# The plain block of a sequence DFT, reordered from re-then-im into two rounds over the halves of d

## The chip, the cores and the metric

The kernel runs on one core of one Trainium2 chip. The metric is the device time of one execution in microseconds, as the median of several runs. The engines are named as the profile names them: PE (TensorE, matmul) with PEld (its weight loads), DVE (VectorE), ACT (ScalarE), POOL (GpSimd) and SP (SyncE, which issues most of the DMAs here).

## The reference

One block of a network on a sequence of S = 2048 tokens with D = 1024 channels, F = 3584 hidden units and one vector c. Every number is f32.

```python
mod = (silu(c) @ w_mod).reshape(1, 6, 1, D)        # w_mod is [1024, 6 * 1024]
sa, ca, ga, sb, cb, gb = (mod[:, i] for i in range(6))
h = layernorm(x) * (1 + ca) + sa
x = x + ga * real(DFT_seq(DFT_hidden(h)))          # two dense DFT matrices, re and im each
h = layernorm(x) * (1 + cb) + sb
x = x + gb * (gelu(h @ w1 + b1) @ w2 + b2)
```

The sequence DFT needs h, and h needs sa and ca, which are two of the six columns of blocks of w_mod: 8 MB of weights stand before the first useful matmul. ga, sb, cb and gb are needed later.

## The kernel before, in words

Every f32 operand of a large product is split into two f16 numbers, a high half and a low half (what the high half misses), and a product is three passes of f16 matmuls, `PASSES = ((0,0),(0,1),(1,0))`, each 128x128 by 128x512. The high half is an ACT copy, the low half a DVE subtraction that waits for it.

The stages follow one another on PE: the plain block of the sequence DFT (its line is L1121, 768 matmuls), then the rest of the sequence DFT in Winograd form (L1171, 2016 matmuls, product operands from DRAM tensors named s and from sums of the planes of c, L725), the hidden DFT (L1403, 1344 matmuls), w1 (L1597) and w2 (L1706), 2352 matmuls each. From 949 us on, w1 and w2 take turns in blocks of 84 to 168 matmuls.

*The plain block* computes, for the first quarter of t, both planes (re and im) of the sequence DFT of all 1024 columns of h. Its loop has 16 steps n = (ri, kp): all eight kp of re, then all eight of im. In a step stand 48 matmuls, for two halves s of the sequence, eight columns of 128 of h (d) and three passes. Eight PSUM banks hold the eight d. A step needs h of row pair kp (rows kp and kp + 8 of the 16 blocks of 128 tokens) and one operand c of 512 KB, split into halves by L690 (ACT) and L693 (DVE). Banks are emptied by ACT at L1100 into a tensor from which the u operands of the hidden DFT are made (sums at L797, high halves at L782, low halves at L785) and stored to DRAM by POOL's queue (L787); u of re is pushed when re is finished, in the middle of the block, and u of im at its end.

*Ahead of it*, sa and ca are made from w_mod by eight loads of 1 MB (`wm2`, loaded at L1436, from SP). Some of them are multiplied on PE with silu(c) broadcast (L482, L483; f32 matmuls), the others by DVE into an accumulator (`mod_dve`, L488, L490), which PE then adds up over the partitions (L496). `mod_rows` finds the largest magnitude (L516), makes a scale from it, and brings the first row block of x to h in two halves (L503, L508; ACT's copies at L521 to L534). `x_tasks` does the same for the other row blocks: the statistics by ACT with an accumulator (L610, L614; each instruction is followed by a read-out of the accumulator), a chain of operations on two columns (L612 to L627), then x minus mean times ca and plus sa over all 1024 columns (L642, L643), the ACT copy (L644) and the low half (L645).

*Beside the block*, `s_tasks` (L652) makes sums and differences of the rows of h over DVE (L656 to L659), splits them (L667, L670) and stores them to s by POOL's DMA queue (L674); they are pushed during im's half. `row_tasks` (L541) does ga, sb, cb and gb: accumulations of 1 MB pieces by DVE (L553), a POOL reduction over the partitions (L561), and a store to a DRAM row by SP (L575), spread over the Winograd blocks. The s operands come back by SP (L752), on the same queue as those stores, as the w_mod loads (L545) and as the loads of c (L714).

*What sets the order.* The kernel is written out by a planner, engine by engine. A piece of work is a `Task` with an engine, an estimated cost, dependencies and a key; `push` puts tasks on named streams with due times, `fill_to(t)` writes out tasks whose estimated end lies before PE's clock, `pick` takes the one that can begin first among those due, and `emitted` and `need` force tasks that the next instruction depends on. `LAGS` and `LANDS` are the delays that the planner adds. The planner's clocks are estimates: on the chip each engine runs its list in order and waits where an operand isn't there. SBUF places are fixed offsets in one tile ("arena"), so a load into a place must wait for the last reader of what was there.

*The w2 operands.* The first w2 block takes seven loads `("w2", 0, m)` of w2's part-products m from DRAM, pushed with tag `w2_0` at L1901 to L1911 in the branch g == 1, and issued by SP at L1907. All seven wait for the z operations (L405, L407, L420) of block NB − 2, whose places they take, and stand behind the stores of w in SP's queue. hid1 is the second half of the hidden activations for that block (`hid_tasks(1)`, L395 on ACT and L407 on DVE).

## Time and profile before

| | us |
|---|---|
| runs | 1980.77, 1979.91, 1982.81 (median 1980.77) |
| the profiled execution's own time | 1980.77 |
| its span in the profile | 1979.0 |
| PE busy | 1950.1 |
| DVE busy | 1426.8 |
| ACT busy | 851.6 |
| POOL busy | 189.3 |
| first matmul of the plain block | 35.39 |
| first matmul of the Winograd part | 209.66 |
| first matmul of the first w2 block | 1010.34 |

How to read it: the span runs from the first to the last recorded event, and the little of the execution that lies outside it is the difference between its own time and the span. Busy times are sums over instructions, so that an engine which is busy for all but a per cent of the span sets the time, and others matter only where it waits for them. A row of the timeline gives start, duration, engine, line, operation, output and inputs, shape and count, and in brackets the idle time of that engine just before, with what ended it. A row of groups gives the busy sum, the mean of one in ns, and the idle time ahead of the group.

### The profile page before, as it was taken

To read this page: it belongs to the slowest core of one execution; us is meant where nothing else is said; L and a number is where in the kernel's file an instruction comes from. 1 tells how busy PE (TensorE), PEld (TensorE's weight loads), DVE (VectorE), ACT (ScalarE), POOL (GpSimd) and SP (SyncE) were. 2 spreads that over 40 slices of the span, in tenths; PEclk is the share of its full clock that TensorE was granted. 3 is DMA by queue.
4 is the path that set the end of the run, shared out by engine and by line. 5 is a ranking of instruction groups with operands and counts; after the bars stand their busy time and mean duration, and the time that the engine had idled before them with its cause. 6 is when DMAs were issued, how large, how long until landed. Compare 5 with 4: busy or idle time off the path is not lost.

```text
span 1979.0 us, 23588 instructions
## 1 busy us (share of the span) xinstructions
PE 1950.1 (99%) x9004; PEld 887.6 (45%) x9004; DVE 1426.8 (72%) x1799; ACT 851.6 (43%) x1091; POOL 189.3 (10%) x282
## 2 busy tenths in 40 slices
PE   7999999999999999999999999999999999999999
PEld 2444444444444444444444444444444444444443
DVE  5977886898984477776689998989873453553566
ACT  4743432445542255554577466456323312312311
POOL 0012211221210012211020000000000000000000
PEclk8999999999999999999999999999999999999999
DMA  9147588688688867878765455344476432432323
GB/s 386 61 163 269 193 283 301 227 331 313 239 287 323 307 230 263 280 239 307 294 216 192 155 182 176 124 159 168 175 222 201 123 102 75 129 102 68 112 75 85
DMA packets 139362, 402.41 MB, mean 203 GB/s; under 512 B 15536, under 2 KB 15536, under 8 KB 134640
## 3 DMA queue, kind: packets, MB, share of 16 engines
q1 hardware_dynamic: 112528, 309.92, 45.6%
q0 software_dynamic: 26720, 90.98, 13.0%
q8 instruction: 70, 1.15, 0.2%
q14 instruction: 44, 0.36, 0.1%
HBM read 262.95 MB, written 137.89 MB: 203 GB/s over the span
## 4 chain that ended last, share of the span: by engine, by line
PE 83%; DVE 10%; DMA 5%; issue 1%; ACT 1%; SPq 0%; DVEq 0%; POOL 0%; ACTq 0%; POOLq 0%
PE ps L1597 24%; PE ps L1706 24%; PE ps L1171 14%; PE ps L1403 14%; PE ps L1121 5%; DVE arena L693 2%; DMA arena<-in_wm_dram 2%; DVE arena L642 1%; DVE arena L643 1%; DMA arena<-s 1%; DMA arena<-u 1%; DVE arena L797 1%; PE ps L1305 1%; DVE arena L645 1%; DVE arena L725 1%
## 5 line engine op out<-in xcount | busy, mean ns | idle before, releaser
L1706 PE MATMUL ps<-arena 128*128 128x512 f16 x2352 | 512.3, 380 | 5.2 <-DMA arena<-w 4.1
L1597 PE MATMUL ps<-arena 128*128 128x512 f16 x2352 | 510.2, 379 | 0.0
L1171 PE MATMUL ps<-arena 128*128 128x512 f16 x2016 | 435.6, 379 | 1.4 <-DMA arena<-s 1.4
L1706 PEld LDWEIGHTS <-arena 128*128 128x128 f16 x2352 | 230.4, 98 | 284.9 <-issue 7.9
L1597 PEld LDWEIGHTS <-arena 128*128 128x128 f16 x2352 | 230.1, 98 | 276.9
L1752 DVE SCALAR_TENSOR_TENSOR arena<-ps,i4c,arena 128x1024 f32<-128x1024 f32 x179 | 229.3, 1281 | 148.9 <-PE ps L1706 144.3
L1171 PEld LDWEIGHTS <-arena 128*128 128x128 f16 x2016 | 197.1, 98 | 239.8 <-DMA arena<-s 2.4
L1403 PE MATMUL ps<-arena 128*128 128x512 f16 x1344 | 292.4, 379 | 0.9 <-DMA arena<-u 0.9
L395 ACT ACTIVATE arena<-arena,shc 128x512 f16<-128x512 f32 (+1 forms) x115 | 116.2, 1018 | 282.6 <-PE ps L1706 190.9
L1403 PEld LDWEIGHTS <-arena 128*128 128x128 f16 x1344 | 131.4, 98 | 157.0 <-DMA arena<-u 1.4
L1121 PE MATMUL ps<-arena 128*128 128x512 f16 x768 | 169.3, 382 | 9.0 <-ACT arena L526 3.9
L420 DVE TENSOR_TENSOR arena<-arena 128x512 f32<-128x512 f32 (+1 forms) x228 | 171.0, 753 | 4.1
L690 ACT ACTIVATE arena<-arena 128x1024 f16<-128x1024 f32 x100 | 104.1, 1050 | 147.3 <-PE ps L1171 110.0
L407 DVE SCALAR_TENSOR_TENSOR arena<-arena,shc 128x512 f16<-128x512 f32 (+1 forms) x115 | 128.6, 1122 | 35.0 <-ACT arena L395 34.6
L693 DVE SCALAR_TENSOR_TENSOR arena<-arena 128x1024 f16<-128x1024 f32 x100 | 128.7, 1304 | 18.9 <-ACT arena L690 18.9
L1623 DVE TENSOR_TENSOR arena<-arena,ps 128x512 f32<-128x512 f32 x84 | 57.6, 685 | 111.8 <-PE ps L1597 107.6
L1616 ACT ACTIVATE arena<-arena,b1s,i1c 128x512 f32<-128x512 f32 x84 | 68.3, 813 | 137.1 <-DVE arena L1623 137.1
L1121 PEld LDWEIGHTS <-arena 128*128 128x128 f16 x768 | 75.2, 98 | 103.5 <-issue 5.6
L782 ACT ACTIVATE arena<-arena 128x1024 f16<-128x1024 f32 x56 | 57.8, 1048 | 60.9 <-DMA u<-arena 21.8
L395 ACT ACTIVATE arena<-arena,s1c 128x512 f16<-128x512 f32 (+1 forms) x70 | 60.7, 884 | 42.3 <-DVE arena L420 30.1
L785 DVE TENSOR_TENSOR arena<-arena 128x1024 f16<-128x1024 f32 x56 | 66.9, 1218 | 14.8 <-ACT arena L782 14.8
L407 DVE SCALAR_TENSOR_TENSOR arena<-arena,s1c 128x512 f16<-128x512 f32 (+1 forms) x70 | 66.2, 959 | 11.3 <-ACT arena L395 11.2
(161 smaller groups left out, 1392.3 us busy)
## 6 DMA issues: line engine op xcount, KB each, us to landing
w<-arena SPq DMA_DIRECT2D x64, 512.0 KB, 4.5
arena<-w SPq DMA_DIRECT2D x119, 256.0 KB, 2.7
u<-arena POOLq DMA_DIRECT2D x56, 512.0 KB, 5.1
arena<-u SPq DMA_DIRECT2D x112, 256.0 KB, 4.1
arena<-w SPq DMA_DIRECT2D x56, 512.0 KB, 3.5
arena<-s SPq DMA_DIRECT2D x48, 512.0 KB, 7.7
arena<-in_cre_dram SPq DMA_DIRECT2D x32, 512.0 KB, 6.8
arena<-in_cim_dram SPq DMA_DIRECT2D x32, 512.0 KB, 5.8
```

What stands on the lines that cost most here:

```text
L395: act.activation(o[m][0], q(j), AF.Copy, **sc)
L407: dve.scalar_tensor_tensor(o[m][1], q(j), scale, o[m][0], op0=ALU.mult, op1=ALU.subtract)
L420: dve.tensor_tensor(q(d), q(a), q(b), op=op)
L690: h = Task("act", 1.15, lambda: act.activation(o[:, :, 0], s2, AF.Copy, scale=SC), list(deps) + free)
L693: dve.scalar_tensor_tensor(o[:, :, 1], s2, SC, o[:, :, 0], op0=ALU.mult, op1=ALU.subtract)
L1121: pe.matmul(bank_of(d_), hleft(d_, s, kp, a), cop(n)[:, s, b], start=(kp == 0 and s == 0 and a == 0 and b == 0), stop=(kp == 7 and s == 1 ...
L1171: pe.matmul(bank_of(st + ch), left, cop(n)[:, s, b], start=(start and kp == 0 and s == 0 and a == 0 and b == 0), stop=(kp == 3 and s == 1 ...
L1403: pe.matmul(bank_of(bk), up(N)[:, c_, a], dp(n)[:, c_, w], start=(start and ri == 0 and c_ == 0 and i == 0), stop=(ri == 1 and c_ == 3 and ...
L1597: pe.matmul(ps.rearrange("p (k t) -> p k t", k=4), w1c[:, m, s, a, d * P : (d + 1) * P], zc(m)[:, b, :, d, :], start=(start and d == 0 and ...
L1616: act.activation(dst, src, AF.Gelu_apprx_tanh, scale=inv, bias=b1s[:, 2 * p + j : 2 * p + j + 1])
L1706: pe.matmul(t[:, j], hidc[:, c_, m, a, k * P : (k + 1) * P], w2c[:, m, c_, w], start=(start and c_ == 0 and n == 0), stop=(c_ == 1 and n = ...
L1752: lambda: dve.scalar_tensor_tensor(dst, ps[b], inv, dst, op0=ALU.mult, op1=ALU.add), kp[b],
```

## The change

It has two parts that don't touch one another.

1. The plain block runs in two rounds q = 0, 1, one per half of d. In a round every kp is passed with re (banks 0 to 3) and im (banks 4 to 7), 24 matmuls each, kp from 0 to 7 in round 1 and from 7 to 0 in round 2. Both rounds need c of re and im: there are places for 10 more than before, and three kp (six operands) are loaded and split again in round 2, so 22 c operands instead of 16. h is made by halves: `h_tasks(k, q)` for each half of the columns. w_mod's sa and ca columns are loaded by halves of d too (512 KB pieces with runs of 2 KB): the first half before the first matmul, as before but with its own scale, the second half by `mod_tasks`, in round 1: eight loads, eight DVE accumulations (L508, L510), a POOL reduction and a chain that ends in the second scale. The evictions multiply by a scale that depends on the half (`esc`). Statistics (`stat_tasks`) are separate from h, and ACT makes them for row pair 0 too. The s operands are made in round 2 (`s_tasks`, kp from 7 to 0), and u of re and im follow the block, im 50 us after re by the planner's due times. 32 dummy f16 matmuls on a constant tile (`idle_pe`), in five groups, stand on PE between the mod matmuls and the first real one. The planner's start time T0 is 23 instead of 42.
2. w2's first operands are pushed one stage sooner (g == 0). Load m = 0 waits for nothing of z(NB − 2), m = 1 for it, and those with m > 2 for hidden activations of the last block; two of z(NB − 2)'s places move to offsets 28 and 30 and one to 196, and hid1's tenth task waits for z(NB − 2). A load of gb waits for both z.

The core of the diff:

```diff
+    def load_wm2(k, q):
+        dst = wm2(k, q).rearrange("p (c d) -> p c d", c=2)
+        sp.dma_start(dst, wm[:, k, 0 : 2 * D].rearrange("p (c h d) -> p c h d", c=2, h=2)[:, :, q, :])
+    def idle_pe(n):
+        w = ones.bitcast(F16)
+        for _ in range(n):
+            pe.matmul(mbank(5), w[:, 0:P], w[:, 0:512], start=True, stop=True)
...
+    def mod_tasks():
+        t = []
+        for k in range(ND):
+            l = Task("dma", 1.3, lambda k=k: load_wm2(k, 1), [("m1", k - 4)] if k > 3 else [], ("wm1", k))
+            t.append([l])
+            f = lambda k=k: mod_dve(mrow, k, 1, k == 0)
+            t.append([Task("dve", 1.3, f, [l.key] + ([("m1", k - 1)] if k else []), ("m1", k))])
...
+        c_ = chain(
+            ("pool", 7.0, lambda: gp.partition_all_reduce(mrow, mrow, P, RED.add)),
+            ("dve", 0.4, one),
+            ("dve", 3.2, top),
+            ("act", 0.65, lambda: act.activation(sas[:, H[1]], mrow[:, H[0]], AF.Copy, scale=sh(1))),
+            ("act", 0.65, lambda: act.activation(ca1s[:, H[1]], mrow[:, H[1]], AF.Copy, scale=sh(1))),
+        )
...
-        t[0].deps = (("h", k, 0), ("h", k, 1), ("op", 4))
+        t[0].deps = (("h", k, 0, 1), ("h", k, 1, 1))
...
-        b = at(O_AUX + 4 * (n % 4), 1024)
+        b = at(32 + 4 * ((7 - n) % 8) if n < 16 else O_AUX + 4 + 4 * (n % 2), 1024)
...
+        f = lambda: act.activation(uf[:, ri, q, c_], bank_of(4 * ri + c_), AF.Copy, scale=esc(ri, q))
...
-        for n in range(16):
-            ri, kp = divmod(n, 8)
-            steps = [(d, s) for s in range(2) for d in range(ND)]
+        for q in range(2):
+            for kp in (range(8), range(7, -1, -1))[q]:
+                all_ = [(d, s) for s in range(2) for d in range(4)]
...
+                    units += [(q, kp, ri, all_) for ri in range(2)]
+        for q, kp, ri, steps in units:
...
-            if n % 8 == 7:
+            if q and last:
                 d = [[("ev", 0, ri, 4 * h + k) for k in range(4)] for h in range(2)]
-                push("u", "u", u_tasks(0, ri, d), clk["pe"] + 40.0 + 20.0 * ri)
+                push("u", "u", u_tasks(0, ri, d), clk["pe"] + (0.0,50.0)[ri])
...
+    order = [("w", k) for k in range(3)] + [("x", 0)] + [("w", k) for k in range(3, 8)] + [("c", 0), ("x", 8), ("c", 1)]
+    order += [("x", 1), ("x", 9), ("c", 2), ("c", 3), ("x", 2), ("x", 10), ("c", 4), ("c", 5)]
...
+    for k in range(7, -1, -1):
+        push("h1", "x", h_tasks(k, 1), t_two(k) - 12.0)
+        push("s", "s", s_tasks(k), t_two(k)+4.0)
...
+    for k in range(3, 8):
+        if k == 4:
+            push("ml", "ml", wl)
+        push("xl", "xl", [load_x(k), load_x(k + 8), c0[2 * k][0], c0[2 * k + 1][0]])
...
-        return at((O_W if b == NB - 1 else 144) + 4 * n, 1024)
+        return at(O_W + 4 * n if b == NB - 1 else 196 if (b, n) == (NB - 2, 0) else 144 + 4 * n, 1024)
...
+                push("w2l", "w2_0", [Task("dma", 1.5, w2_f(m), [("kept", NB - 1, 0)] if m > 2 else [("z", NB - 2, j) for j in range(7)] if m == 1 else [], ("w2", 0, m)) for m in (0, 1, 2, 4, 3, 6, 5)], due[4, 0] - 10.0)
...
-                push("hid", "hid1", hid_tasks(1), due[4, 0])
+                h1 = hid_tasks(1)
+                h1[9].deps += tuple(("z", NB - 2, m) for m in range(7))
+                push("hid", "hid1", h1, due[4, 0])
```

402 lines of the change are left out of this document (207 added, 195 removed).

## Prediction, written before the changed kernel had been run

> **What bounds the kernel now.** I read the page's first line and section 1, then TensorE's rows in the timeline. The run in which the profile was taken lasted 1980.77 us beside a span of 1979.0, so 1.77 us lie around the span; its time is also the median of the three runs, so the sum is made against 1980.77 directly.
>
> ```profile
> span 1979.0 us, 23588 instructions
> PE 1950.1 (99%) x9004; PEld 887.6 (45%) x9004; DVE 1426.8 (72%) x1799; ACT 851.6 (43%) x1091; POOL 189.3 (10%) x282
> ```
>
> TensorE is busy for all but 1979.0 − 1950.1 = 28.9 us, and the change leaves the count of real matmuls as it is (768 in the plain block in either order). So only two things can move the end: a gap on PE, or a stretch in which PE runs at half pace. The timeline shows where these are (columns: start, duration, what, then idle time before and its releaser):
>
> ```profile
> 35.39 1.16 PE L1121 MATMUL ps<-arena 128*128 128x512 f16 x2 [3.86 <-ACT arena L526]
> 37.66 6.60 PE L1121 MATMUL ps<-arena 128*128 128x512 f16 x23 [0.20 <-DVE arena L503]
> ...
> 52.67 62.75 PE L1121 MATMUL ps<-arena 128*128 128x512 f16 x290 [1.07 <-DVE arena L693]
> ...
> 209.66 93.40 PE L1171 MATMUL ps<-arena 128*128 128x512 f16 x432
> 304.24 119.31 PE L1171 MATMUL ps<-arena 128*128 128x512 f16 x552 [1.18 <-DMA arena<-s]
> 987.95 18.29 PE L1597 MATMUL ps<-arena 128*128 128x512 f16 x84
> 1010.34 38.18 PE L1706 MATMUL ps<-arena 128*128 128x512 f16 x168 [4.09 <-DMA arena<-w]
> 1048.35 36.42 PE L1597 MATMUL ps<-arena 128*128 128x512 f16 x168
> ```
>
> There are three places. The start: no matmul of the DFT before 35.39. The plain block: the pace is 36.42/168 = 0.217 us a matmul (0.2158 from start to start), so 768 take 165.7 us, but the block lasts 209.66 − 35.39 = 174.3; it loses 8.6. The first w2 block: 4.09 us of waiting for its operands, and then 38.18 instead of 36.42 for the same 168 matmuls, a loss of 1.8 to the clock, which had fallen in the gap. A gap of 1.07 (at 52.67) leaves the pace alone, one of 3.86 (at 35.39) is followed by 23 matmuls in 6.60 us (5.0 at full pace).
>
> The other engines, by stretch (columns: PE, PEld, DVE, ACT and POOL busy, then clock, DMA share, GB/s):
>
> ```profile
> 53.00:118.00 65.00, 63.55 (x295) 28.48 (x293) 62.22 (x87) 41.58 (x62) 1.27 (x1) 1.00 0.21 66
> 118.00:210.00 92.00, 92.00 (x428) 41.70 (x427) 64.48 (x70) 40.54 (x48) 21.31 (x39) 1.00 0.72 242
> 209.66:304.24 94.58, 93.40 (x434) 42.18 (x432) 79.03 (x62) 34.05 (x34) 17.19 (x10) 1.00 0.72 253
> 1067.00:1084.60 17.60, 17.60 (x83) 7.95 (x82) 17.43 (x21) 14.83 (x20) 0.00 (x0) 1.00 0.64 207
> ```
>
> In the first half of the plain block DVE is all but full (62.22 of 65): a block that asks for h and c sooner finds no free DVE there.
>
> **Step 1, the start.** Half of w_mod (512 KB pieces) is loaded before the first matmul instead of all of it (1 MB pieces).
>
> ```profile
> 7.13 3.36 PE L483 MATMUL ps<-arena 128*128 128x512 f32 x4 [7.13 <-DMA arena<-in_wm_dram]
> 9.57 1.29 DVE L488 TENSOR_SCALAR arena<-arena,scol 128x2048 f32<-128x2048 f32 x1 [8.13 <-DMA arena<-in_wm_dram]
> 12.04 2.35 DVE L490 SCALAR_TENSOR_TENSOR arena<-arena,scol 128x2048 f32<-128x2048 f32 x1 [1.18 <-DMA arena<-in_wm_dram]
> 28.31 1.06 ACT L690 ACTIVATE arena<-arena 128x1024 f16<-128x1024 f32 x1 [0.70 <-DMA arena<-in_cre_dram]
> 28.99 0.69 DVE L516 TENSOR_REDUCE mx<-ps 128x1 f32<-128x512 f32 x1 [0.59 <-PE ps L496]
> 34.70 0.63 ACT L526 ACTIVATE arena<-arena 128x512 f16<-128x512 f32 x1 [0.96 <-DVE arena L508]
> 37.64 0.75 DVE L508 SCALAR_TENSOR_TENSOR arena<-arena,xcl 128x512 f32<-128x512 f32 x1
> ```
>
> Two 1 MB pieces that DVE waits for come 12.04 − 9.57 = 2.47 apart, so 512 KB take 1.24 us. PE's first matmul waits for piece 0 until 7.13 in the trace of before, so piece 0's first half is there at about 5.9. Piece 7 is the ninth transfer (x0 lies between): 5.9 + 8 × 1.24 = 15.8; c0 follows at 17.1, x8 at 18.3. I take it that the new runs of 2 KB keep this rate, as the c0 load, which has runs of that length, already does (it ends ACT's wait at 28.31, in its turn). The accumulations of 0.75 per 512 columns, in their place between x0's statistics, end at about 18.9. Then ACT, in this order, brings half of x0 to its mean and scale (0.63, to 19.75), makes c0's high half (1.06) and adds up x8 (1.06 and 0.19, rows below). The small DVE operation that takes that sum stands ahead of the first reduction on DVE, so it is what ends last: 19.75 + 1.06 + 1.25 = 22.1. Then two reductions and two sums over 512 columns (4 × 0.6 from start to start) and four operations on one column (about 0.2 each) give the scale at D0 = 25.3. An ACT copy of 0.63 follows, and the first real matmul runs at **26.1 instead of 35.39**: 9.3 us earlier. Twelve of the 32 dummy matmuls run just before it, so it starts at full pace.
>
> **Step 2, round 1.** Here this head start is spent. In a round each kp takes 48 × 0.2158 = 10.36 us for re and im together, and needs a new h (halves of d) and two new c operands. Before, it needed whole h and one c in that time. The price list, per 1024-wide row:
>
> ```profile
> L693 DVE SCALAR_TENSOR_TENSOR arena<-arena 128x1024 f16<-128x1024 f32 x20 | 24.1, 1217 | 0.0
> L643 DVE SCALAR_TENSOR_TENSOR arena<-arena,xcl 128x1024 f32<-128x1024 f32 x15 | 19.2, 1282 | 0.3
> L645 DVE TENSOR_TENSOR arena<-arena 128x1024 f16<-128x1024 f32 x15 | 18.3, 1223 | 3.5 <-ACT arena L644 3.5
> L627 DVE SCALAR_TENSOR_TENSOR xcl<-xcl,m 128x2 f32<-128x2 f32 x7 | 1.5, 219 | 0.1
> L614 ACT ACTIVATE arena<-arena,xcl 128x1024 f16<-128x1024 f32 x14 | 16.0, 1142 | 0.2
> L610 ACT ACTIVATE arena<-arena 128x1024 f16<-128x1024 f32 x12 | 12.6, 1047 | 0.2
> L614 ACT ACTIVATION_READ_ACCUMULATOR arena<-arena,xcl 128x1 f32 x14 | 2.6, 187 | 0.0
> 329.12 7.01 POOL L561 PARTITION_ALL_REDUCE arena<-arena  x1 [34.12 <-DVE arena L553]
> 330.08 5.56 DVE L725 TENSOR_TENSOR arena<-arena 128x1024 f32<-128x1024 f32 x1
> ```
>
> A kp now costs DVE 4 half-wide operations (0.73 each), one low half of h and two of c (1.14 each from start to start), and some eight small ones: 7.5 us of 10.36. ACT has 8 to 8.5 (four statistics of 1.2 with their read-outs, three copies of 1.0, a root). That fits. What does not is the second half of w_mod, which stands in the same round: eight accumulations of about 1.21, and one POOL reduction over 1024 columns. While such a reduction runs in the trace of before, a DVE operation with two SBUF operands takes 5.56 instead of 1.21: DVE stands for 4.35 us. Its first piece can't be worked on before it lands; it is the 36th transfer, 5.9 + 35 × 1.24 = 49.4 = D0 + 24.1.
>
> Counting DVE's new order from D0, four h's matter. The low half of kp 1's h is there at D0 + 16.7 (12 us of work, the rest waits for ACT's statistics); kp 2's stands behind two accumulations, 24.1 + 2 × 1.21 + 1.14 = 27.7. By kp 3's, seven accumulations lie ahead (8.5), two low halves of h and one of c (3.4), four half-wide operations (2.9) and a dozen small ones (2.4): 24.1 + 17.2 = 41.3. To kp 4's come three low halves of c (3.4), one accumulation (1.2), five half-wide operations (3.6), one low half (1.1), small ones (2) and the POOL reduction (4.35): 41.3 + 15.7 = 57. From there PE still has four kp: 57 + 4 × 10.36 = 98.5. Kp 1 alone would allow 16.7 + 72.5 = 89, kp 3 93, kp 5 (63.6) 95. Unhindered the round would end at D0 + 83.7; so about 14.8 us of gaps arise, more than twice those of before.
>
> Round 2 takes 82.9 us. Statistics and w_mod are done by then, the s operands (ACT 1.05, DVE four half adds and 1.22 twice, stores on POOL) move into it, and I see 8.5 to 9.5 us of DVE per kp against 10.36, behind h that is ahead by about 10: no gap. The 82.9 us hold two 4-bank groups whose evictions lie behind the other group's matmuls. The block then ends at 25.3 + 98.5 + 82.9 = 206.7 against 209.66: **−3.0**. The unknown in it is DVE's order: if no small operation waits, kp 4 is ready 2 sooner; if ACT's copies come late behind statistics, 3 later. Range for the block's end: 203.5 to 209.5.
>
> On the gaps: the one before 35.39 was 3.86 and cooled the clock, that of 1.07 did not. Those I expect before kp 1, 3 and 4 are 2.5 to 3.5, in between. One that cools costs 1.6 on the 23 matmuls that took 6.60 and 0.7 on the two ahead of them, which took 1.16: about +2.4, inside the range. The Trainium skill ("TensorE: Matmul & The Clock Gate", "What's actually happening") says that the clock falls to half after an idle window of about 3.4 us that runs free of the program, and rises after as much work; the rows at 35.39 and 1010.34 agree, and it speaks against the change, since by it each of these gaps might, or might not, cool: 209.1 for the block's end with one. The page "SBUF — State Buffer" of the Trainium skill ("Who interferes with whom") has the lock, and would let the whole reduction of 7.01 block DVE; the row at 330.08 shows 4.35, and by the page the end would be 2.7 later.
>
> **Step 3, behind the block.** Before, u of re was made during im's half; now u of re and im come after the block. The trace before has seven u low halves and four sums of re inside the block:
>
> ```profile
> arena<-s SPq DMA_DIRECT2D x48, 512.0 KB, 7.7
> L785 DVE TENSOR_TENSOR arena<-arena 128x1024 f16<-128x1024 f32 x7 | 8.3, 1217 | 0.0
> L797 DVE TENSOR_TENSOR arena<-arena 128x1024 f32<-128x1024 f32 x4 | 4.9, 1218 | 0.0
> 243.77 0.33 SPq L575 DMA_DIRECT2D row_ga<-arena  x1
> 256.47 0.33 SPq L752 DMA_DIRECT2D arena<-s  x1
> 295.03 0.33 SPq L575 DMA_DIRECT2D row_sb<-arena  x1
> 296.10 1.15 SPq L752 DMA_DIRECT2D arena<-s  x1
> ```
>
> About 12 us of DVE work land in a stretch with 94.58 − 79.03 = 15.6 free. It just fits: cost between −1.2 (the present gap at 304.24 goes, because row_sb's store, for which the s load behind it on SP waited, moves back in SP's order) and +12 (rival D). The nearest row is that gap of 1.18; I take +0.5.
>
> **Step 4, w2's first operands.** m = 0 is no longer behind z and is loaded with w1's, so it lies in SBUF when w1's first block ends at 1006.24. m = 1 still waits for z of the second last block:
>
> ```profile
> 1004.30 0.68 DVE L405 TENSOR_TENSOR arena<-arena 128x512 f16<-128x512 f32 x1
> 1005.01 9.84 SPq L1907 DMA_DIRECT2D arena<-w  x7
> 1006.30 1.28 DVE L407 SCALAR_TENSOR_TENSOR arena<-arena,shc 128x1024 f16<-128x1024 f32 x1
> ```
>
> z is done at 1004.98, SP issues at 1005.01, and the first operand released PE at 1010.34: 5.3 us. Now 24 matmuls of m = 0 (5.2 us) lie in that time. The low half of hid1 that they need is done at 1007.58, so 1.3 of the wait stay. 4.09 + 1.8 − 1.3 = **−4.6**; I take −4.5 (at least −3, if m = 1 is 1.5 late; at most −5.8, if hid1 is early too).
>
> **Sum:** −3.0 + 0.5 − 4.5 = −7.0, so 1980.77 − 7.0 = **1973.8 us**. Own range: −3.0 within +3 and −3, the others within +1.3 and −2: about 1969 to 1978.5.
>
> **Rivals.**
> - **B, round 1 isn't starved.** If the mod operations find their place in DVE's free time, the gaps of 14.8 shrink to about 5 and the block ends at 197: 1980.77 − 12.7 + 0.5 − 4.5 = 1964. For it: 7.5 of 10.36 per kp. Against it: 62.22 of 65 in the present half.
> - **C, w2's gain is given back.** DVE has 17.43 of 17.60 at 1067 to 1084.6; if DVE, not PE, sets the pace to there, the earlier start only becomes a wait in the next w2 block: 1980.77 − 3.0 + 0.5 = 1978.3. For it: that row. Against it: DVE's queue moves forward with hid1 as well.
> - **D, slower.** Place: SP's queue in the first Winograd block. Two s loads (for the fifth product operand) stand behind row_ga's store there, which waits for DVE's last operation on that row; that operation moves behind u of re and im. The third load is needed after 14 groups of 24 matmuls, 72.5 us after the block's start, and lands some 7.7 after issue: if DVE gets to the row later than 64 us after the block's start (34 now, 243.77 − 209.66), PE stands for the excess. 34 + 12 leaves 18 of slack; with the whole u work and w_mod's waits ahead of it, 76 would be a stall of 12: 1973.8 + 12 = 1986.
>
> **How the numbers follow.** Forecast 0.45, B 0.22, C 0.13, D 0.20. About 0.2%, 4 us, is what a measurement of this kernel tells from no change: faster is below 1976.8, slower above 1984.7. Faster: 0.40 of the forecast's 0.45 and all of B, 0.62. Same: the rest of the forecast 0.05, C 0.13 and 0.02 of D, 0.20. Slower: 0.18. The range reaches down over B, to 1961, and up to 1984, which leaves out most of D and a little of B.
>
> **What would show it.** First real matmul at 26.1 (step 1); gaps on PE before kp 1, 3 and 4, released by DVE's low halves, with the largest sum in round 1, and a DVE operation of 5.5 us beside POOL's reduction (step 2); no gap in round 2, and the first Winograd matmul at 206 to 207; no gap over 2 us between there and 304 (step 3), else D; the first w2 matmul about 1.3 after w1's last, and m = 1 without a wait (step 4); no new wait for DVE in the w2 block after it, else C. The forecast is wrong most easily in step 2, by the count of DVE's work between D0 and kp 4.

## The result and the profile after

The changed kernel is slower: 1991.51 us in the median of five runs (1988.72 to 1992.79) against 1981.65 of before (1979.91 to 1982.81), a ratio of 1.0043 with a 95% interval of 1.0031 to 1.0055. The profiled execution took 1991.13 us beside a span of 1989.4; the span of before is 1979.0, so the traces differ by 10.4 us, and that is the sum to be explained.

The first line and section 1 of the page of after:

```profile
span 1989.4 us, 23674 instructions
PE 1948.3 (98%) x9006; PEld 885.5 (45%) x9006; DVE 1450.9 (73%) x1868; ACT 868.0 (44%) x1116; POOL 196.8 (10%) x283
```

PE has as much to do as before (1948.3 against 1950.1: 17.9 us instead of 23.7 ahead of the plain block, and more in slow stretches behind gaps), and stands 41.1 instead of 28.9 us. DVE has 24 us more. Where PE stands, the timeline of after shows (start, duration, what, idle time before and its releaser):

```profile
25.41 5.50 PE L1148 MATMUL ps<-arena 128*128 128x512 f16 x24 [1.33 <-ACT arena L1517]
...
39.42 0.61 PE L1148 MATMUL ps<-arena 128*128 128x512 f16 x2 [2.49 <-ACT arena L656]
40.68 10.53 PE L1148 MATMUL ps<-arena 128*128 128x512 f16 x48 [0.66 <-DVE arena L657]
54.65 11.79 PE L1148 MATMUL ps<-arena 128*128 128x512 f16 x46 [3.43 <-DVE arena L657]
...
69.00 11.99 PE L1148 MATMUL ps<-arena 128*128 128x512 f16 x47 [2.00 <-DVE arena L706]
...
83.88 124.06 PE L1148 MATMUL ps<-arena 128*128 128x512 f16 x574 [1.47 <-DVE arena L657]
207.78 52.18 PE L1199 MATMUL ps<-arena 128*128 128x512 f16 x241
260.92 36.42 PE L1199 MATMUL ps<-arena 128*128 128x512 f16 x168 [0.96 <-DVE arena L706]
301.08 12.21 PE L1199 MATMUL ps<-arena 128*128 128x512 f16 x48 [3.74 <-DVE arena L706]
316.04 88.00 PE L1199 MATMUL ps<-arena 128*128 128x512 f16 x407 [2.75 <-DVE arena L706]
409.74 194.04 PE L1199 MATMUL ps<-arena 128*128 128x512 f16 x888 [5.70 <-ACT arena L1218]
605.51 57.15 PE L1199 MATMUL ps<-arena 128*128 128x512 f16 x264 [1.73 <-DMA arena<-s]
662.50 77.86 PE L1431 MATMUL ps<-arena 128*128 128x512 f16 x360
...
1020.94 2.75 PE L1759 MATMUL ps<-arena 128*128 128x512 f16 x12
1025.31 33.85 PE L1759 MATMUL ps<-arena 128*128 128x512 f16 x156 [1.61 <-DMA arena<-w]
1058.99 36.42 PE L1650 MATMUL ps<-arena 128*128 128x512 f16 x168
```

L1148 is the plain block, L1199 the Winograd part, L1431 the hidden DFT, L1650 and L1759 are w1 and w2. Set against the rows of before (its hidden DFT begins at 646.54), stage by stage:

| stage | before, us | after, us | difference | predicted |
|---|---|---|---|---|
| up to the first matmul of the plain block | 35.39 | 25.41 | −10.0 | −9.3 |
| plain block | 174.3 | 182.4 | +8.1 | +6.3 |
| Winograd part | 436.9 | 454.7 | **+17.8** | +0.5 |
| hidden DFT to the end of w1's third block | 359.7 | 358.4 | −1.3 | 0 |
| first w2 block with its wait | 42.1 | 38.05 | −4.1 | −4.5 |
| the rest of the span | 930.6 | 930.4 | −0.2 | 0 |

These are single executions. In the traces of w2_alone, before_plus24 and before_op_2, which start like before, the first matmul runs at 37.6 to 38.2, so the first row is good to some 3 us. The Winograd part repeats better: 436.9 in w2_alone, and 454.5 and 456.2 in mod_quarter and mod_no_wait, which leave it as it is in after.

Everything but one line is within 2 us of the prediction. The Winograd part, whose matmuls the diff leaves as they are, takes 17.8 us more: 14.9 us of gaps and the slow stretches behind two of them (48 matmuls in 12.21 instead of 10.36 at 301.08, 888 in 194.04 instead of 191.6 at 409.74) against 1.4 us of gaps before.

What DVE does ahead of the gap at 301.08, in the timeline of after:

```profile
288.25 1.28 DVE L569 SCALAR_TENSOR_TENSOR arena<-arena,scol 128x1024 f32<-128x1024 f32 x1 [3.19 <-DMA arena<-in_wm_dram]
...
292.55 1.28 DVE L569 SCALAR_TENSOR_TENSOR arena<-arena,scol 128x1024 f32<-128x1024 f32 x1 [1.88 <-DMA arena<-in_wm_dram]
...
297.22 2.67 DVE L569 SCALAR_TENSOR_TENSOR arena<-arena,scol 128x1024 f32<-128x1024 f32 x2
299.81 1.22 DVE L706 SCALAR_TENSOR_TENSOR arena<-arena 128x1024 f16<-128x1024 f32 x1
```

L569 accumulates pieces of w_mod for the row sb, which nothing needs for hundreds of us. Twice DVE stands because a piece hasn't landed, 5.1 us in all, and the low half of an operand (L706), for which PE has stood since 297.3, is queued behind them. A few us on, the gap at 316.04 has the other cause; POOL's rows and DVE's, in the timeline of after:

```profile
309.21 7.28 POOL L577 PARTITION_ALL_REDUCE arena<-arena  x1
```

```profile
310.56 7.70 DVE L706 SCALAR_TENSOR_TENSOR arena<-arena 128x1024 f16<-128x1024 f32 x3
```

Three operand splits, 3.5 us of work, take 7.70 beside the reduction of row sb. The largest gap, 5.70 ahead of 409.74, comes by way of ACT. PE waits for an eviction (L1218, at 408.60), which ACT does behind copies of u (L796) that wait for DVE's sums of u (L811). DVE had stood 2.8 us for pieces, ahead of 385.93 and 388.27, and then beside the reduction of row gb:

```profile
390.61 5.56 DVE L811 TENSOR_TENSOR arena<-arena 128x1024 f32<-128x1024 f32 x1
```

So there are two suspects, waits for pieces (W) and the stand beside reductions (L), and a third, that DVE simply has too much to do (B). The kernel before had the same pieces and the same reductions, and no such gaps. Its DVE even stood longer for pieces, 30.0 us between 208 and 424 where it is 14.3 in after, and once for 10 us on end:

```profile
308.11 0.75 DVE L551 TENSOR_SCALAR arena<-arena,scol 128x1024 f32<-128x1024 f32 x1 [10.20 <-DMA arena<-in_wm_dram]
```

### The profile page after: what moved, and what is told of

It is laid out like the page before. It is cut to its first block, busy times and chain, and to the rows that moved or that the text cites. A ratio compares the mean times of both kernels' runs of the same rounds, so it can differ in the third digit from the quotient of the medians.

```text
span 1989.4 us, 23674 instructions
## 1 busy us (share of the span) xinstructions
PE 1948.3 (98%) x9006; PEld 885.5 (45%) x9006; DVE 1450.9 (73%) x1868; ACT 868.0 (44%) x1116; POOL 196.8 (10%) x283
## 4 chain that ended last, share of the span: by engine, by line
PE 82%; DVE 8%; DMA 6%; issue 2%; ACT 2%; SPq 0%; POOL 0%; DVEq 0%; ACTq 0%; POOLq 0%
PE ps L1759 24%; PE ps L1650 23%; PE ps L1431 15%; PE ps L1199 13%; PE ps L1148 6%; DMA arena<-in_wm_dram 3%; DVE arena L706 2%; DVE arena L569 1%; DVE arena L739 1%; DVE arena L408 1%; PE ps L1333 1%; DMA arena<-s 1%; DVE arena L510 1%; DVE arena L811 0%; DVE arena L799 0%
## 5 line engine op out<-in xcount | busy, mean ns | idle before, releaser
L1759 PE MATMUL ps<-arena 128*128 128x512 f16 x2352 | 510.8, 379 | 2.7 <-DMA arena<-w 1.6
L1650 PE MATMUL ps<-arena 128*128 128x512 f16 x2352 | 510.2, 379 | 0.0
L1199 PE MATMUL ps<-arena 128*128 128x512 f16 x2016 | 440.0, 381 | 14.9 <-DVE arena L706 7.5
L1759 PEld LDWEIGHTS <-arena 128*128 128x128 f16 x2352 | 230.0, 98 | 281.2 <-issue 3.1
L1650 PEld LDWEIGHTS <-arena 128*128 128x128 f16 x2352 | 230.1, 98 | 276.9
L1199 PEld LDWEIGHTS <-arena 128*128 128x128 f16 x2016 | 198.1, 98 | 256.6 <-issue 19.6
L1431 PE MATMUL ps<-arena 128*128 128x512 f16 x1344 | 292.2, 379 | 0.0
L1431 PEld LDWEIGHTS <-arena 128*128 128x128 f16 x1344 | 131.5, 98 | 155.9
L1148 PE MATMUL ps<-arena 128*128 128x512 f16 x768 | 171.0, 384 | 12.9 <-DVE arena L657 5.6
L703 ACT ACTIVATE arena<-arena 128x1024 f16<-128x1024 f32 x106 | 109.6, 1049 | 143.8 <-PE ps L1199 103.7
L706 DVE SCALAR_TENSOR_TENSOR arena<-arena 128x1024 f16<-128x1024 f32 x106 | 139.8, 1330 | 33.0 <-ACT arena L703 33.0
L1148 PEld LDWEIGHTS <-arena 128*128 128x128 f16 x768 | 75.2, 99 | 108.6 <-issue 7.2
L796 ACT ACTIVATE arena<-arena 128x1024 f16<-128x1024 f32 x56 | 57.8, 1049 | 85.2 <-DMA u<-arena 38.0
```

Of the source, the lines that this page charges most:

```text
L703: h = Task("act", 1.15, lambda: act.activation(o[:, :, 0], s2, AF.Copy, scale=SC), list(deps) + free)
L706: dve.scalar_tensor_tensor(o[:, :, 1], s2, SC, o[:, :, 0], op0=ALU.mult, op1=ALU.subtract)
L1148: pe.matmul(bank_of(4 * ri + d_), hleft(4 * q + d_, s, kp, a), cop(n)[:, s, b], start=(first and s == 0 and a == 0 and b == 0), stop=(last ...
L1199: pe.matmul(bank_of(st + ch), left, cop(n)[:, s, b], start=(start and kp == 0 and s == 0 and a == 0 and b == 0), stop=(kp == 3 and s == 1 ...
L1431: pe.matmul(bank_of(bk), up(N)[:, c_, a], dp(n)[:, c_, w], start=(start and ri == 0 and c_ == 0 and i == 0), stop=(ri == 1 and c_ == 3 and ...
L1650: pe.matmul(ps.rearrange("p (k t) -> p k t", k=4), w1c[:, m, s, a, d * P : (d + 1) * P], zc(m)[:, b, :, d, :], start=(start and d == 0 and ...
```

## The experiments

The measure in all of them is the length of the Winograd part in the profile, from its first matmul to that of the hidden DFT: 436.9 us before, 454.7 after. The total is named where it was timed in rounds.

**w2_alone**: before, with the second part of the change alone.

> The kernel before with part 2 alone: w2's first operands loaded one stage sooner, the plain block as before. Theory: the two parts are independent, and part 2 is worth what the changed kernel shows between the end of w1's third block and the start of the next w1 block: 42.1 us before, 38.05 after, so -4.1, about 1977.6. Nothing up to 1006 us should move. Rival: part 2 shifts DVE's z and hid work so that the gain is taken back in the following blocks; then within 1 us of before.

Measured: 1978.32 us against 1981.98 of before, ratio 0.998 (0.997 to 0.9989). Its rows at the first w2 block:

```profile
1008.52 2.75 PE L1706 MATMUL ps<-arena 128*128 128x512 f16 x12
1012.46 34.27 PE L1706 MATMUL ps<-arena 128*128 128x512 f16 x156 [1.19 <-DMA arena<-w]
1046.56 36.42 PE L1597 MATMUL ps<-arena 128*128 128x512 f16 x168
```

38.04 us instead of 42.1. The second part is a gain of 4 us by itself, it isn't taken back, and this kernel beats both. The whole loss is the first part's.

**rows_later**: the changed kernel with the row tasks moved back.

```diff
-        push("row", "row", row_tasks(...), t_op(22) + 20.0 + 30.0 * n)
+        push("row", "row", row_tasks(...), t_op(22) + 60.0 + 45.0 * n)
```

> The changed kernel with one thing moved: the due times of the four w_mod row tasks (ga, sb, cb, gb) go from 20 + 30 n to 60 + 45 n us after the plain block's end. Theory B (backlog: DVE enters the Winograd part with some 25 us more work than before and is the bound for 200 us): work that isn't urgent leaves the full stretch, the gaps at 301, 316 and 410 go, the Winograd part shrinks from 454.7 to about 440 us, total 1976 to 1979. Theory S (the second round's s operands or SP's queue come too late, whatever DVE does): the Winograd part stays over 450 us, total 1989 to 1992.

Measured: 1991.32 us (ratio to before 1.0048, 1.0031 to 1.0064), Winograd part 449.9. Neither theory had it: the gaps at 261 to 316 are gone and that of 410 shrank to 0.85, but new ones came:

```profile
208.03 186.64 PE L1199 MATMUL ps<-arena 128*128 128x512 f16 x864
395.53 41.60 PE L1199 MATMUL ps<-arena 128*128 128x512 f16 x192 [0.85 <-ACT arena L1218]
441.60 13.36 PE L1199 MATMUL ps<-arena 128*128 128x512 f16 x48 [4.47 <-DMA arena<-s]
455.94 5.35 PE L1199 MATMUL ps<-arena 128*128 128x512 f16 x24 [0.98 <-DMA arena<-s]
464.71 193.36 PE L1199 MATMUL ps<-arena 128*128 128x512 f16 x888 [3.41 <-DMA arena<-s]
```

So the row work does make the early gaps, and it makes others where it is put. Of the 4.8 us that the part is shorter, 4.2 are lost again behind it: from the hidden DFT's first matmul (657.91) to the first w2 block (1020.52) it takes 362.6 us instead of 358.4.

**rows_later_pool**: the same, with the stores of the rows issued by POOL instead of SP (`gp.dma_start` for `sp.dma_start` in `put`).

> The changed kernel with the row tasks later (60 + 45 n) and their five stores issued from POOL's queue instead of SP's. With the row tasks later alone the gaps up to 410 were gone, but 8.9 us came back at 441 to 465, released by s loads. Theory Q (those s loads stood on SP behind the stores of row gb and gbb, which wait for POOL's reduction and for DVE): the gaps at 441 to 465 go, the Winograd part takes 438 to 442 us, total 1976 to 1980. Theory R (the ring of s loads or the DMA engines are late there anyway): they stay, total 1988 to 1992.

Measured: 1989.22 us (ratio 1.0034, 1.0022 to 1.0047), Winograd part 447.6, with 2.07 at 449.81 and 5.69 at 460.85 left, released by s loads. Theory Q explains little over 2 us: the prediction's rival D (s loads behind row stores on SP) is real, but small, and the rest of that trouble is not the stores' place. Both traces show where it comes from. DVE stands for row gb's last operation (L588), 11.89 us ahead of 438.79 in rows_later and 9.87 ahead of 436.87 in rows_later_pool, because that operation comes behind a reduction of 9.32 us and a transfer. The splits queued behind it are late, the loads of c wait for the places that these splits free, and the s loads stand behind the loads of c in SP's queue.

**rows_narrow**: DVE's work on the rows nearly gone, its waits kept. Seven of eight accumulations run over 16 columns:

```diff
-  dve.scalar_tensor_tensor(mrow, b, scol[:, k : k + 1], mrow, op0=ALU.mult, op1=ALU.add)
+  dve.scalar_tensor_tensor(mrow[:, 0:16], b[:, 0:16], scol[:, k : k + 1], mrow[:, 0:16], op0=ALU.mult, op1=ALU.add)
```

> The changed kernel with the accumulations of ga, sb, cb and gb over 16 of 1024 columns for seven of eight pieces (the rest of those rows is left out); loads, reductions and the order stay. Theory B (backlog): 28 operations of 1.28 us become 0.1 to 0.2, so DVE has about 30 us back in the 200 us after the plain block; the gaps at 301, 316 and 410 go and the Winograd part takes 438 to 442 us. Theory W (DVE stands in its queue for w_mod pieces that land late, 5.3 us to 318 and 8.3 after): the waits stay, so at least the gap at 301 of 3.7 us stays, and the part takes over 446 us.

Measured: 445.9 us. The windows of this run (PE, PEld, DVE, ACT, POOL busy, then clock, DMA share and GB/s) and its PE rows:

```profile
260.00:318.00 58.00, 51.23 (x233) 22.73 (x231) 42.98 (x41) 19.92 (x20) 10.93 (x8) 0.98 0.81 291
```

```profile
299.01 5.34 PE L1199 MATMUL ps<-arena 128*128 128x512 f16 x24 [1.22 <-DVE arena L706]
306.36 5.34 PE L1199 MATMUL ps<-arena 128*128 128x512 f16 x24 [2.01 <-DVE arena L706]
315.24 281.39 PE L1199 MATMUL ps<-arena 128*128 128x512 f16 x1295 [3.54 <-DVE arena L706]
```

Half of the loss came back (8.8 of 17.8 us), which is between the two theories. DVE is busy 43 of 58 us here, and PE still stands 6.8 us for it, with a quarter of DVE's time free. So work has a part in the loss, but the half that is left isn't a want of DVE time: that speaks for waits, W, against B alone.

**lock_short**: the four reductions over 32 of 1024 columns, every instruction in its place.

> The changed kernel with the four POOL reductions of ga, sb, cb and gb over 32 of 1024 columns (the rest isn't reduced); every instruction stays in its place. Theory L (the reductions, during which DVE stands 4.35 us each, make the gaps): the gap of 2.75 at 316 and most of the 5.70 at 410 go, the one of 3.7 at 301 stays; the Winograd part takes about 445 us. Theory B (backlog): the three reductions ahead of 410 give DVE 13 us back, which is worth something at every later gap; 443 to 448 us. By B the gap at 301, which has one reduction ahead of it, must shrink too.

Measured: 441.0 us. The gap at 316 is gone, 2.94 at 301.29 and 0.70 at 307.33 are left, and that of 410 is gone too. That is more than either theory had.

**no_piece_wait** and **no_wait_no_lock**: seven of the eight accumulations of each row read `mrow` in place of the piece `b`, so that only a row's first piece is still waited for (0.8 us of waits up to 320 in the first run, 2.1 in the second); the second has the short reductions too.

> The changed kernel in which seven of the eight accumulations of each of ga, sb, cb and gb read the row that they add to instead of the w_mod piece (the pieces are loaded and not used, so those rows are left out); the order, the size of every DVE operation, the traffic and the reductions stay, and only the wait for a piece's landing goes. The run with the 12 us of u work off DVE gave back 2.1 us in the Winograd part (452.6 instead of 454.7), so a sum of work is not what binds. Theory W (DVE stands in its queue for pieces that land 8 to 10 us after their issue, with operand splits behind): the gap at 301 goes with its slow stretch (5.6 us), that of 410 shrinks; the part takes 443 to 449 us. Theory B2 (backlog): with the same DVE work it stays over 452.

> The same, and POOL's four reductions over 32 of 1024 columns (the rest is left out). The short reductions alone gave a Winograd part of 443.1 us, with gaps of 2.9 at 301 and 0.7 at 307 left and about 2 us of slow clock behind them. Theory W and L together (waits for pieces, and the stand of DVE beside reductions, are the whole of the loss): the part takes 436 to 439 us, as before the change, with no gap over 1.5 us before 590. If it stays over 441, a third cause is left.

Measured: 440.9 without the waits, 437.3 without both. Of the early gaps, 1.05 at 261.62 and 2.80 at 311.20 are left in the first run and none in the second. An s load's gap that after has too (1.73 at 605.51) stays in both; it is 2.03 at 588.71 in the second, where none over 1.5 was expected. (The expectation took lock_short's part from the block's end in after; from its own, 209.91, it is the 441.0 above.) W alone is worth 13.8 us, L alone 13.7, both 17.4: they overlap, because either is enough to use up the same lead. With both gone the part takes what it took before the change (436.9). The windows of no_wait_no_lock show that DVE's work is all there:

```profile
208.38:320.00 111.62, 111.62 (x519) 50.59 (x518) 102.18 (x91) 47.42 (x49) 13.86 (x22) 1.00 0.82 303
```

And the same for after:

```profile
207.78:318.00 110.22, 102.77 (x468) 46.02 (x467) 102.46 (x84) 45.43 (x47) 24.91 (x22) 0.98 0.74 265
```

DVE is busy 102 of 112 us with 91 operations, and PE runs without a gap; in after DVE is busy as long with 84, and PE has 102.8 of 110. Work alone (B) isn't the cause; that is shown.

**u_re_on_act**: the term that the prediction priced, u of re, taken off DVE (low halves by ACT, sums over 32 columns).

> The changed kernel with the first block's re operands of u taken off DVE: the seven low halves are ACT copies and the four sums run over 32 of 1024 columns (so those values are left out); 11 x 1.13 = 12.4 us of DVE work less behind the plain block, which is the term that the prediction counted for step 3. Theory B2 (backlog and lost lead): the gaps at 301, 316 and 410 shrink to half or less, the Winograd part goes from 454.7 to 443 to 448 us. Theory W (waits for w_mod pieces alone): it stays over 451.

Measured: 452.6. Twelve us of DVE work less gave 2.1. Groups of DVE, 209.41 to 319.6 in this run:

```profile
L569 DVE SCALAR_TENSOR_TENSOR arena<-arena,scol 128x1024 f32<-128x1024 f32 x14 | 18.0, 1282 | 9.7 <-DMA arena<-in_wm_dram 9.3
...
L567 DVE TENSOR_SCALAR arena<-arena,scol 128x1024 f32<-128x1024 f32 x1 | 0.8, 753 | 4.8 <-DMA arena<-in_wm_dram 4.8
```

The same groups in after, 207.78 to 318:

```profile
L569 DVE SCALAR_TENSOR_TENSOR arena<-arena,scol 128x1024 f32<-128x1024 f32 x14 | 17.9, 1279 | 5.5 <-DMA arena<-in_wm_dram 5.3
...
L567 DVE TENSOR_SCALAR arena<-arena,scol 128x1024 f32<-128x1024 f32 x1 | 0.8, 773 | 0.7 <-DMA arena<-in_wm_dram 0.7
```

DVE waits for pieces 14.1 instead of 6.0 us: most of the time that was freed turned into standing at the same places of its queue.

**before_plus24**: the reverse, the kernel before with small DVE work added behind the block. It was to be as much as the change moved there, but the 80 additions took 37.2 us: some 29 by themselves, the rest as two stands beside reductions.

> The kernel before with 80 small DVE additions (192 columns, about 0.3 us each, some 24 us) added in the first 110 us behind the plain block, four behind each of the first 20 operand splits; all else as before. Theory B2 (the changed kernel loses time because about 24 us of DVE work that used to lie ahead of the block's end now lies behind it, and eats the lead that hid DVE's waits for w_mod pieces and reductions): this kernel, too, gets gaps on PE at 280 to 420, released by DVE's operand splits, and the Winograd part grows from 436.9 to 446 to 455 us. Theory O (it is the new order of the instructions, not their sum): it stays under 440 us.

Measured: 456.0, +19 us, with 6.25 at 302.53 and 8.86 at 323.40, released by s loads and not by splits as was expected. So more work on DVE in that stretch does cost time, as long as the waits and reductions are there. The way is another one. The s load that ended the 8.86 was issued at 315.99, right behind a load of c that had waited at 315.56 for the place that a split freed at 315.53. The one that ended the 6.25 was issued at 293.94 behind a piece's load, at 293.56, whose place an accumulation freed at 293.53. SP issued its loads in order in these rows, so a late DVE held it up.

**before_op_2**: the kernel before with the operand splits set later in DVE's order, nothing else.

```diff
-                push("op", "op", op_tasks(tb, m, kp), t_op(n) - 15.0)
+                push("op", "op", op_tasks(tb, m, kp), t_op(n) + 2.0)
```

> The kernel before with one number changed: the operand splits of the Winograd part are due 2 us behind their planned use instead of 15 ahead of it, so that the planner sets them late in DVE's order. Sum of DVE's work, traffic, pieces and reductions stay. Theory H (lead hides: before the change every split was done 12 to 27 us ahead of its matmuls up to 345 us, and that alone covered DVE's waits for pieces and its stand beside reductions; after it the lead is 0 to 16): the Winograd part grows from 436.9 to 445 us or more, with gaps released by splits behind piece waits or reductions. Theory N (the waits of the kernel before lie elsewhere in the order and would hit nothing): it stays under 440.

Measured: 466.1, +29 us, with every large gap released by a split. Rows of PE and of DVE in this run:

```profile
283.51 7.03 PE L1171 MATMUL ps<-arena 128*128 128x512 f16 x24 [3.62 <-DVE arena L693]
293.52 95.09 PE L1171 MATMUL ps<-arena 128*128 128x512 f16 x432 [2.99 <-DVE arena L693]
399.62 54.13 PE L1171 MATMUL ps<-arena 128*128 128x512 f16 x240 [11.01 <-DVE arena L693]
```

```profile
278.77 1.28 DVE L553 SCALAR_TENSOR_TENSOR arena<-arena,scol 128x1024 f32<-128x1024 f32 x1 [2.55 <-DMA arena<-in_wm_dram]
...
282.24 1.22 DVE L693 SCALAR_TENSOR_TENSOR arena<-arena 128x1024 f16<-128x1024 f32 x1
...
284.51 7.82 DVE L725 TENSOR_TENSOR arena<-arena 128x1024 f32<-128x1024 f32 x3
292.26 6.89 DVE L693 SCALAR_TENSOR_TENSOR arena<-arena 128x1024 f16<-128x1024 f32 x6
```

The split at 282.24 stands behind a wait for a piece, those at 292.26 behind three sums that take 7.82 beside a reduction. The kernel before has waits and stands of these two kinds as well; what keeps them off PE is that its splits are done early. The largest gap, 11.01 at 399.62, has a third kind, which before hasn't: DVE stands 10.85 us, up to 394.93, for row gb's last operation (L572), as in rows_later. How early is to be counted from two rows of groups, the first of before up to 209.66, the second of after up to 207.78:

```profile
L693 DVE SCALAR_TENSOR_TENSOR arena<-arena 128x1024 f16<-128x1024 f32 x20 | 24.1, 1217 | 0.0
```

```profile
L706 DVE SCALAR_TENSOR_TENSOR arena<-arena 128x1024 f16<-128x1024 f32 x23 | 27.7, 1218 | 6.9 <-ACT arena L703 6.9
```

Sixteen of the 20 belong to the plain block, 22 of the 23 in after. So before has four operands, 4 × 24 × 0.2158 = 20.7 us, ahead of PE when the Winograd part begins, and after has one, 5.2 us. Matching the splits with their groups of 24 matmuls one by one gives a lead of 9 to 27 us at every group up to 325 us before the change, and at most 16 after it, down to nothing where the gaps at 261, 301 and 316 are. In no_wait_no_lock the lead is as short (0.8 us at 255, about 2 at 302), and PE doesn't stand: it takes a short lead and a wait together. The count at the border isn't enough by itself, either: before_op_2 still has three operands ahead there (19 splits).

**op_40** and **op_40_later**: the attempt to buy the lead back by due times (`t_op(n) - 40.0` for the splits), the second with the rows later too.

> The changed kernel with the due times of the Winograd part's operand splits 40 us ahead of their use instead of 15, so that the planner sets them ahead of row work in DVE's order where their ring of six places allows. All the work stays. Theory P (the splits' lead is what matters: at the block's end one split lies ahead where it was four before the change): the gaps at 301 and 316 go or fall under 1 us; the Winograd part takes 440 to 447 us, total 1977 to 1984. Theory W alone without the lead: the same waits hit other work that is urgent as well (u, c sums), and the part stays at 450 to 456.

> Both: the splits' due times 40 us ahead, and the row tasks at 60 + 45 n. Theory P: the trouble that the later rows alone had at 441 to 465 us (8.9 us of waits for s loads behind row stores on SP) is no operand split, so it stays, and the part takes 444 to 450 us, as with the later rows alone (449.9). If it falls under 441, DVE's order was at the bottom of that trouble too, by way of u and the c sums.

Measured: 453.2 and 444.8. Theory P in this form fails in the first; the second is in its range, but its gaps (4.00 at 401.27, 2.27 at 547.57) are released by evictions on ACT and not by s loads. By the same counting, op_40 has five operands ahead at the block's end, but it has a gap of 6.25 at 314.34, released by a split's high half on ACT, which had stood 9.93 us for a sum of the c planes on DVE; that sum in turn is queued behind a wait for a piece (2.73 at 303.73). What has to lead is the whole chain from plane to operand, and a due time for its last step moves the trouble one step up. op_40_later comes to 1981.88 us in its single run (1980.94 of before beside it). With the second part's 4 us counted, the first part's loss falls from some 14 us to some 5 by two due times, but there is no gain in it.

**pieces_pool** and **pieces_act**: the 32 loads of pieces from another engine's queue.

> The changed kernel with the 32 loads of w_mod's pieces for ga, sb, cb and gb issued from POOL's queue instead of SP's; all work stays. Theory Q2 (pieces land late because their loads stand on SP behind s loads that wait for PE): DVE's waits for pieces shrink, the Winograd part falls to 443 to 449 us. Theory T (they land late because of the traffic, 8 to 10 us from issue whatever the queue, or POOL's own order holds them up): 452 to 460.

> The same with the loads issued from ACT's queue. ACT is busy 45 of the first 110 us and stands where a piece's place isn't free yet. Theory Q2: 441 to 449 us for the Winograd part. Theory T: 452 or more; if ACT's stand holds up high halves, up to 465.

Measured: 465.6 and 451.0. SP's queue is at most a small part of what makes the pieces late. From ACT's, DVE waits 10.7 us for pieces between 208 and 424 instead of 14.3, and the Winograd part is 3.7 us better. From POOL's, in whose order reductions and u stores stand, it waits 22.8, and the part is 11 worse.

**mod_quarter** and **mod_no_wait**: round 1. The first shortens six of eight accumulations of w_mod's second half to 16 columns; the second keeps their size, but reads data that is there already, and has a short reduction.

> The changed kernel with six of the eight DVE accumulations of w_mod's second half over 16 of 1024 columns (that part of sa and ca is left out); loads and order stay. By the prediction's step 2 (round 1 is held up by DVE's sum of work up to the fifth row pair) 6 x 1.1 = 6.6 us come back in round 1, and the plain block ends at about 201 instead of 207.8. If round 1's gaps come from ACT's copies or from landings, it ends at 205 or later. The Winograd part should stay at 452 to 457.

> The changed kernel with w_mod's second half not read in round 1: its eight accumulations read other data of the same size that is there already, and the reduction runs over 32 of 1024 columns (that half of sa and ca is left out). DVE's work stays. Theory W and L in round 1: DVE's waits for pieces (3.5 at 52.7, 1.4 at 67) and its stand beside the reduction (4.4 at 71) make the gaps at 54.6, 69 and 84 and the slow stretches behind them; the block ends at 198 to 201 instead of 207.8. Step 2 of the prediction (the sum of DVE's work): it ends at 203 or later, since only 4.35 us of the 14.8 were the reduction.

Measured, from the first matmul of the block to its end: 182.5 us for mod_quarter, 176.9 for mod_no_wait, 182.4 for after. Taking 6.6 us of work away gave nothing; taking the waits and the reduction away gave 5.4.

## Why the prediction was wrong, step by step

**Step 1** was right: the first matmul runs at 25.41 (26.1 forecast), released as worked out, by the chain from x8's first sum. (Its sum is 0.2 us generous in two places: 18.9 + 0.63 is 19.5 and not 19.75, 25.3 + 0.63 is 25.9 and not 26.1.)

**Step 2** was right in size and mostly wrong in its reason. The block ends at 207.78 (206.7), with 16.6 us more than its matmuls need, where 14.8 of gaps were forecast. Of the 16.6 only 11.4 are gaps, and most of the rest is slow stretches, which the forecast had left out of the sum: that the sizes agree is partly luck. The step counted DVE's work up to the fifth row pair (kp 4), and mod_quarter shows that the work of the accumulations isn't what binds. Waits for pieces of w_mod and the reduction together are 5.4 (mod_no_wait). The 2.49 at 39.42, which comes before the second half of w_mod is there at all, waits for an ACT copy; the cause of the other 9 or so wasn't tested. The reduction was priced from a row of before, and that held. In after:

```profile
71.26 4.50 DVE L625 TENSOR_TENSOR xcl<-xcl 128x2 f32<-128x2 f32 x1
```

**Step 3** is the step that failed. It said that about 12 us of DVE work "land in a stretch with 94.58 − 79.03 = 15.6 free. It just fits". Two things were wrong in it. The smaller: the work that moved behind the block is more than u: with three operand splits and three sums of c planes that used to be done ahead, and the last s operands, it is some 24 us by the groups. The larger: the 15.6 us weren't free. The same window's groups in before are

```profile
L693 DVE SCALAR_TENSOR_TENSOR arena<-arena 128x1024 f16<-128x1024 f32 x18 | 30.1, 1696 | 0.7 <-ACT arena L690 0.7
L553 DVE SCALAR_TENSOR_TENSOR arena<-arena,scol 128x1024 f32<-128x1024 f32 x14 | 17.9, 1278 | 8.5 <-DMA arena<-in_wm_dram 8.4
```

so 8.5 of the 15.6 us were waits in an in-order queue, during which what is queued behind can't run; and 8.2 us that count as busy were stands beside two reductions (18 splits alone take 18 × 1.217 = 21.9). The sum of work is also not what sets the loss: PE runs through with the same 102 us of work when nothing waits (no_wait_no_lock). What the change took away is the lead of the operands, 20.7 us down to 5.2 at the block's end, and that lead covered waits of up to 3.3 us, the one of 10.20 and stands of 4.4 us. before_op_2 shows it in the kernel before with one number, no_wait_no_lock in the kernel after. The step cost 17.8 us where 0.5 was forecast; these 17.3 are all that lies between the forecast of 1973.8 and the 1991.13 of the trace, since the other steps' errors cancel. The upper bound given for this step, +12, was the price of rival D, and too low.

**Step 4** was right to half a us (−4.1 for −4.5), with one detail wrong: load m = 0 feeds 12 matmuls (2.75 us at 1020.94) and not 24, so m = 1 is waited for (1.61); the low half of hid1, for which 1.3 us had been allowed, costs nothing here. That the two come out alike is luck.

**The rivals.** B (round 1 not starved) and C (w2's gain given back) are out: the gap ahead of the next w2 block's later part is 0.47 in after and 0.40 before. D had the place, the first Winograd block behind a DVE that is late, and the sign, at 12 us; but its mechanism, s loads behind row_ga's store on SP, isn't the one: no gap up to 410 is released by an s load. It showed only when the rows were moved (rows_later), and moving the stores took back 2 us of it. D was near in one thing: in before_plus24 and the two rows_later runs s loads do stand in SP's queue behind what a late DVE holds up, but that is loads of c and pieces more than a row's store.

**What stays open**: how the waits of DVE for pieces could be had shorter (the queue is at most a small part, pieces_act and pieces_pool); what makes the rest of the loss in round 1; and how the 19 us of before_plus24 divide between the additions and the stands. A version of the first part that keeps the lead wasn't found; the best of the kernels run that leave nothing out is w2_alone.

## What to carry to other kernels

Idle time of an in-order engine is free only if nothing is queued behind the wait; before filling it, read from the groups how much of it is a wait, and for what. What keeps such waits off the critical engine is the lead of its operands, so a change that moves work across a stage's border is to be priced in lost lead against the longest stand of the engine that makes them. The operands ready at the border, times the time that one feeds, are a first count; op_40 had five ready and still lost 16 us, so the lead has to be followed along the whole stretch. Work that isn't urgent, with a wait or a lock in it, can be dear in a queue that also feeds the bound, well beyond its busy time.

## What the runs showed of the hardware

A reduction on POOL held DVE up for as long with an operation on two columns as with one on 1024. In after, the operation on two columns above took 4.50 us instead of 0.15; the one at 390.61 took 5.56 instead of 1.21. Between 75.7 and 76.0, with the same reduction of 6.99 us that began at 70.35 still running, three small operations took 0.15 to 0.16 each. Two more, each with one tensor operand, then took over a us until the reduction was over:

```profile
75.98 1.38 DVE L627 TENSOR_SCALAR xcl<-xcl 128x2 f32<-128x2 f32 x1
76.10 1.26 DVE L624 RECIPROCAL xcl<-xcl 128x2 f32<-128x2 f32 x1
```

The Trainium skill ("SBUF — State Buffer", "Who interferes with whom") has the stand for DVE operations with two SBUF inputs, which agrees with the 4.50. For one input outside the two-port modes it says that there is none, but it names tensor_scalar, the first of these two rows, among the operations that can enter such a mode. The second row may have stood behind the first in DVE's order, so the rows decide nothing here.

The clock fell after gaps shorter than the 3.86 us of before. In after, 47 matmuls behind the gap of 2.00 at 69.00 took 11.99 us, where 47 in lock_short take 10.30 at full pace; the granted clock was 0.72 from 69 to 75. In lock_short, 24 behind a gap of 2.94 took 5.34, none more, at a clock of 1.00. The same place of the same instruction order came out both ways: behind the gap of 2.49 at 39.42, 48 matmuls took 10.53 us in after, and in rows_later_pool

```profile
40.51 11.95 PE L1148 MATMUL ps<-arena 128*128 128x512 f16 x48 [0.66 <-DVE arena L657]
```

That agrees with a window that runs free of the program, as the Trainium skill has it ("TensorE: Matmul & The Clock Gate", "What's actually happening"); its figure of about 3.4 us isn't a length that a gap must reach here.
